# Eight loads of a decode attention kernel whose last bytes go as DMAs of fewer rows

## The chip, the core and the metric

The kernel runs on one core of one Trainium2 chip. The metric is the device time of one execution in microseconds, the median of several runs. Lower is better.

## The reference

Two attention blocks are computed for one decoded token, and their results are mixed by a gate. Block A has 16 heads with a K and a V cache each; block B has 16 query heads that share 8 K and V heads. Each cache is 8192 positions by 256 numbers, all in float32. The query is x (448 numbers) times wq, and the heads' outputs go through wo back to 448 numbers.

```python
def _A_ref(x, k_cache, v_cache, wq, wo):
    q = (x @ wq).reshape(B, Sq, H, Dh).transpose(0, 2, 1, 3)
    scores = jnp.einsum("bhqd,bhkd->bhqk", q, k_cache) * (Dh ** -0.5)
    p = _softmax(scores, axis=-1)
    o = jnp.einsum("bhqk,bhkd->bhqd", p, v_cache)
    return o.transpose(0, 2, 1, 3).reshape(B, Sq, H * Dh) @ wo

# Eight loads of a decode attention kernel whose last bytes go as DMAs of fewer rows
g = _sigmoid((x * gate_w).sum(-1, keepdims=True))
return g * _A_ref(x, ...) + (1 - g) * _B_ref(x, ...)
```

Each byte of the caches and weights is used once, so all 432 MB have to come from HBM into SBUF.

## The kernel before, in words

The host lays all caches and weights into one array, `stream`, in the order in which they are used. There are eight steps s. A step handles two heads of A (r = 0 and 1) and one K and V head of B (r = 2) with its two query heads. `order()` writes the order of the items by hand: wq of a step, four K tiles and four V tiles for each r, and wo. A tile is 128 partitions by 4096 numbers.

The stream is cut without regard to the items into 54 loads (`fills()`): 52 of `FILL` = 15872 numbers (63488 bytes) a partition, and two at the end (`TAIL`) that are cut into four pieces each, of 5632, 4096, 4096 and 1920, and of 1344, 896, 336 and 112 numbers. A `UNIT` is 512 numbers, 2048 bytes. `load(n)` takes a tile from a ring of three slots (`SLOTS`) and issues one DMA for each piece from SyncE (SP). Each piece lies in HBM as one contiguous block, row by row: the block's row p goes to partition p. A new load is issued as soon as the last item that reads the oldest slot has been handled, so SP waits for the last reader of the slot. SP issues nothing else but the output at the end.

The consumers take an item by `pieces()`, which splits it where a load or a piece of a load ends; each split item needs one instruction for each part.

- `scores_a` (K of A): VectorE (DVE) multiplies the tile by the broadcast query in place (L234) and sums over 256 numbers (L235).
- `scores_b` (K of B), `queries` (wq), `attend` (V) and `emit` (wo): TensorE (PE) matmuls, all of them by the helper at L96.
- `softmax`, `take` and `narrow` are short steps on all engines after a head's last tile.

After the last item the kernel adds up the last output row: `emit_last` copies Y, the last blocks of matmuls follow, and the result goes to HBM from four partitions in one DMA of 4 rows (L412).

A DMA has one of eight completion counters, taken in turn. The ninth DMA waits on SP until the first has landed, and so on.

In the profile the load is L112, and its tile is `slot<-in_stream_dram`.

Of the kernel before, what the change touches and what calls it, by code (L numbers as in the profile page):

```python
# [14 lines left out]
P = 128  # L15
# [13 lines left out]
UNIT = 2 * DH  # L29
# [2 lines left out]
WO = 4 * 2 * D  # L32
FILL = 31 * UNIT
SLOTS = 3
TAIL = [[11 * UNIT, 8 * UNIT, 8 * UNIT, 2 * UNIT + 896], [1344, 896, 336, 112]]


def order():

    out = [("wq", 0, 0, 0)]  # L40
    for s in range(NS):
        def k(r, *ts):
            return [("k", s, r, t) for t in ts]

        def v(r, *ts, of=s):
            return [("v", of, r, t) for t in ts]

        if s == 0:
            out += k(0, 0) + k(2, 0, 1) + k(0, 1) + k(2, 2) + k(0, 2) + k(2, 3) + k(0, 3)
            out += v(2, 0, 1) + k(1, 0) + v(2, 2, 3) + k(1, 1) + v(0, 0, 1) + k(1, 2) + v(0, 2)  # L50
            out += k(1, 3) + v(0, 3) + [("wq", 1, 0, 0)]
            continue
        out += k(0, 0) + v(1, 0, 1, of=s - 1) + k(0, 1) + v(1, 2, 3, of=s - 1)
        out += k(0, 2) + k(2, 0, 1) + k(0, 3) + k(2, 2, 3) + [("wo", s - 1, 0, 0)]
        out += k(1, 0) + v(0, 0, 1) + k(1, 1) + v(0, 2, 3)
        if s < NS - 1:
            out += [("wq", s + 1, 0, 0)] + k(1, 2) + v(2, 0, 1) + k(1, 3) + v(2, 2, 3)
        else:
            out += k(1, 2) + v(2, 0) + k(1, 3) + v(2, 1, 2, 3) + v(1, 0, 1, 2, 3) + [("wo", s, 0, 0)]
    return out  # L60
# [5 lines left out]
def fills():  # L66

    total = sum(SIZE[i[0]] for i in order())
    tail = sum(map(sum, TAIL))
    full, rest = divmod(total - tail, FILL)  # L70
    return [[FILL]] * full + ([[rest]] if rest else []) + TAIL


@with_exitstack
def kernel(
# [6 lines left out]
    nc = tc.nc  # L82
    scale = DH ** -0.5

    const = ctx.enter_context(tc.tile_pool(name="const", bufs=1))
    ring = ctx.enter_context(tc.tile_pool(name="ring", bufs=SLOTS))
    small = ctx.enter_context(tc.tile_pool(name="small", bufs=2))
# [9 lines left out]


    FILLS = fills()
    starts, at = [], 0  # L100
    for f in FILLS:
        starts.append(at)
# [4 lines left out]
    def load(n):  # L107
        t = ring.tile([P, FILL], F32, name="slot")
        o = 0
        for size in FILLS[n]:  # L110
            a = (starts[n] + o) * P
            nc.sync.dma_start(t[:, o:o + size], stream[a:a + size * P].rearrange("(p f) -> p f", p=P))  # L112
            o += size
        slots[n] = t

    def pieces(a, n):

        got, end, o = [], a + n, a
        for k, s in enumerate(starts):
            e = s + sum(FILLS[k])  # L120
            if s <= o < e and o < end:
                c = s
                for size in FILLS[k]:
                    if c <= o < c + size and o < end:
# [8 lines left out]
    xs = const.tile([P, 2 * (KF + 1)], F32, name="xs")  # L133
    nc.scalar.dma_start(xs, small_in)
    load(0)
    load(1)
    load(2)

    zero = const.tile([P, UNIT], BF16, name="zero")
# [4 lines left out]
    rows = const.tile([P, 2 * R, NG], F32, name="rows")  # L144
# [24 lines left out]
    for h in range(2):  # L169
        p = slice(h * KR, (h + 1) * KR)  # L170
# [188 lines left out]
    items, a = [], 0  # L359
# [3 lines left out]
    assert a == TOTAL  # L363
    ends = [s + sum(f) for s, f in zip(starts, FILLS)]
    later = {}
# [3 lines left out]

    nxt = SLOTS  # L370
    gone = 0
    last = len(items) - 1
    for i, ((kind, s, r, t), a) in enumerate(items):
# [29 lines left out]
        while gone < len(ends) and a + SIZE[kind] >= ends[gone]:  # L403
            gone += 1
            if nxt < len(FILLS):
                load(nxt)
# [81 lines left out]
```

## Time and profile before

| what | value |
|---|---|
| median of 3 runs | 1013.41 us (1013.23 to 1015.39) |
| the profiled execution | 1013.38 us |
| its span, first to last instruction | 1011.6 us |
| HBM read | 432.02 MB, 427 GB/s over the span |
| busy: PE, DVE, ACT | 535.4, 597.7, 37.6 us |
| DMA packets on SP's queue | 8648, 98.9% of 16 engines' span |
| a full load, from issue to landing, median | 40.4 us |

The profile has a page of sums, the groups of instructions with what ended the idle time before them, the chain of waits that ended last, and, for any stretch of time, the mean busy share of the core's 16 DMA engines and the packets that started in it. A DMA's packets are its rows, and one completion of 4 bytes for each engine that it uses. The packets are not told apart by engine.

### The profile page before, as it was taken

What the parts mean: (1) busy time and instruction counts of PE and PEld (TensorE: products, weight loads), DVE (VectorE), ACT (ScalarE), POOL (GpSimd) and SP (SyncE); (2) the same over time, 40 slices, a digit from 0 to 9 for tenths busy, and PEclk for the clock granted to TensorE, in tenths of its full rate; (3) what the DMA queues carried; (4) which work ended last, traced back from release to release, by engine and by line L of the source; (5) the groups of instructions that cost most, each with busy time, mean ns of one, the idle gap of its engine ahead of it and who ended that gap; (6) DMA issues with size and microseconds to landing.
All of it is one profiled execution on the core that took longest, in us unless ns stands there. A gap on an engine that the chain in (4) does not pass through costs nothing.

```text
span 1011.6 us, 6308 instructions
## 1 busy us (share of the span) xinstructions
PE 535.4 (53%) x2839; PEld 156.0 (15%) x2839; DVE 597.7 (59%) x298; ACT 37.6 (4%) x106; POOL 0.7 (0%) x6
## 2 busy tenths in 40 slices
PE   1715555764628455547325565438554457336647
PEld 0201111120102120112101121102211112102102
DVE  1687775636763488536657635844488447656671
ACT  0000000000000000000000000000000000000000
POOL 0000000000000000000000000000000000000000
PEclk9957776876768676778767877767777778766769
DMA  9999999999999999999999999999999999999996
GB/s 402 440 442 425 422 437 439 437 427 427 434 435 440 429 427 429 437 432 432 432 437 432 428 437 430 435 432 427 437 440 427 425 434 437 437 429 432 427 424 262
DMA packets 8818, 432.42 MB, mean 427 GB/s; under 512 B 1240, under 2 KB 1368, under 8 KB 1752
## 3 DMA queue, kind: packets, MB, share of 16 engines
q1 hardware_dynamic: 8648, 432.02, 98.9%
q8 instruction: 22, 0.36, 0.1%
q10 hardware_dynamic: 144, 0.00, 0.0%
q14 instruction: 4, 0.03, 0.0%
HBM read 432.02 MB, written 0.00 MB: 427 GB/s over the span
## 4 chain that ended last, share of the span: by engine, by line
DMA 62%; DVE 24%; PE 11%; another core or an unknown queue 1%; ACT 1%; issue 0%; SPq 0%
DMA slot<-in_stream_dram 62%; DVE s L235 12%; DVE slot L234 12%; PE sc L96 3%; PE o L96 3%; PE sm L96 2%; PE q L96 2%; PE Y L96 2%; ACT px L277 0%; ACT p L286 0%; SPq L112 0%; DVE least L264 0%; ACT bias L272 0%; DVE low L253 0%
## 5 line engine op out<-in xcount | busy, mean ns | idle before, releaser
L234 DVE TENSOR_TENSOR slot<-slot,q 128x4096 f32<-128x4096 f32 (+5 forms) x80 | 284.7, 3559 | 102.0 <-DMA slot<-in_stream_dram 102.0
L235 DVE TENSOR_REDUCE s<-slot 128x16 f32<-128x4096 f32 (+5 forms) x80 | 285.3, 3567 | 2.8
L96 PE MATMUL o<-slot,p 128*2 128x512 f32 x1024 | 177.3, 797 | 189.8 <-DMA slot<-in_stream_dram 189.8
L96 PE MATMUL sc<-slot,qb 128*32 128x512 f32 x512 | 90.2, 820 | 105.7 <-DMA slot<-in_stream_dram 105.4
L96 PE MATMUL o<-slot,pr 128*4 128x512 f32 x512 | 83.8, 777 | 78.3 <-DMA slot<-in_stream_dram 78.3
L96 PEld LDWEIGHTS o<-slot,p 128*2 128x2 f32 x1024 | 28.8, 99 | 317.9 <-DMA slot<-in_stream_dram 211.2
L264 DVE TENSOR_REDUCE least<-sm 1x1 f32<-1x128 f32 (+1 forms) x24 | 5.8, 243 | 109.2 <-PE sm L96 92.0
L96 PE MATMUL Y<-slot,ocs 128*1 128x448 f32 (+3 forms) x178 | 54.6, 501 | 12.3 <-DMA slot<-in_stream_dram 12.0
L330 DVE TENSOR_TENSOR ocs<-sm,rz 128x2 f32<-128x2 f32 (+1 forms) x24 | 3.7, 154 | 76.8 <-PE sm L96 76.8
L96 PEld LDWEIGHTS sc<-slot,qb 128*32 128x32 f32 x512 | 19.9, 142 | 166.9 <-DMA slot<-in_stream_dram 114.1
L96 PE MATMUL q<-slot,xr 128*128 128x512 f32 (+1 forms) x80 | 35.5, 598 | 0.0
L96 PEld LDWEIGHTS o<-slot,pr 128*4 128x4 f32 x512 | 14.1, 100 | 137.6 <-DMA slot<-in_stream_dram 86.8
L316 ACT ACTIVATE ob<-o 128x512 f32<-128x512 f32 (+1 forms) x24 | 14.1, 588 | 534.7 <-PE o L96 534.7
L96 PE MATMUL sc<-slot,xr 128*1 128x512 f32 (+1 forms) x80 | 28.8, 507 | 0.0
L253 DVE TENSOR_REDUCE low<-sc 128x1 f32<-128x512 f32 x8 | 5.5, 688 | 32.5 <-PE sc L96 32.5
L96 PE MATMUL sm<-pick_a,ob 128*128 128x1 f32 x128 | 19.4, 272 | 5.6 <-ACT ob L316 5.6
L96 PEld LDWEIGHTS sm<-pick_a,ob 128*128 128x128 f32 x128 | 18.0, 217 | 19.2 <-ACT ob L316 16.4
L96 PEld LDWEIGHTS q<-slot,xr 128*128 128x128 f32 x80 | 17.0, 222 | 24.0 <-issue 23.5
L290 DVE RECIPROCAL rz<-sm 128x1 f32<-128x1 f32 (+1 forms) x24 | 4.1, 169 | 27.2 <-PE sm L96 27.2
L96 PE MATMUL sm<-ident,low 128*1 128x128 f32 x48 | 10.8, 312 | 17.6 <-DVE low L238 16.8
L96 PEld LDWEIGHTS Y<-slot,ocs 128*1 128x1 f32 x178 | 11.3, 91 | 49.5 <-issue 36.3
L272 ACT ACTIVATE bias<-sm 128x1 f32<-128x1 f32 x24 | 4.1, 171 | 348.5 <-PE sm L96 348.5
(62 smaller groups left out, 132.8 us busy)
## 6 DMA issues: line engine op xcount, KB each, us to landing
slot<-in_stream_dram SPq DMA_DIRECT2D x52, 7936.0 KB, 40.4
slot<-in_stream_dram SPq DMA_DIRECT2D x2, 2048.0 KB, 32.4
slot<-in_stream_dram SPq DMA_DIRECT2D x1, 2816.0 KB
slot<-in_stream_dram SPq DMA_DIRECT2D x1, 960.0 KB, 36.5
slot<-in_stream_dram SPq DMA_DIRECT2D x1, 672.0 KB, 25.7
slot<-in_stream_dram SPq DMA_DIRECT2D x1, 448.0 KB, 26.5
slot<-in_stream_dram SPq DMA_DIRECT2D x1, 168.0 KB, 26.5
slot<-in_stream_dram SPq DMA_DIRECT2D x1, 56.0 KB, 22.2
```

Of the source, the lines that this page charges most:

```text
L96: nc.tensor.matmul(o, l, r, start=start, stop=stop, skip_group_check=True)
L234: nc.vector.tensor_tensor(v, v, q[:, None, :].to_broadcast([P, n, DH]), op=OP.mult)
L235: nc.vector.tensor_reduce(S[s, r][:, t * ROWS + j:t * ROWS + j + n], v, axis=AX.X, op=OP.add)
L253: nc.vector.tensor_reduce(low, sc, axis=AX.X, op=OP.min)
L264: nc.vector.tensor_reduce(least[:, :m], view, axis=AX.XY if r == 2 else AX.X, op=OP.min)
L272: nc.scalar.activation(bias, all_rows, AF.Copy)
L290: nc.vector.reciprocal(rz[:, :m], z[:, :m])
L316: nc.scalar.activation(ob[:, :n], o[:, :n], AF.Copy)
L330: nc.vector.tensor_tensor(ocs[:, :, :m], oc[:, :, :m], RZ.pop((s, r))[:, None, :m].to_broadcast([P, 2, m]), op=OP.mult)
```

## The change

Eight loads, numbers 30, 32, 34 and so on to 44, are now two pieces. In load 30 the second piece is 10 units (20480 bytes a partition), in the seven others it is one unit (2048 bytes). The first piece is a DMA of 128 rows as before. The second is issued as several DMAs over parts of the partitions (`parts()`): one of 112 rows for partitions 0 to 111, and small ones for the last 16 partitions. In load 30 these are four DMAs of 4 rows. In the seven others they are two, of a and 16 - a rows, with a different pair in each: (12, 4), (10, 6), (9, 7), (13, 3), (14, 2), (15, 1), (11, 5). The same bytes reach the same places of the slots.

```diff
+LOW = 4
+SHARE = 10 * UNIT
+PAIRS = [(12, 4), (10, 6), (9, 7), (13, 3), (14, 2), (15, 1), (11, 5)]
...
-    return [[FILL]] * full + ([[rest]] if rest else []) + TAIL
+    out = [[FILL]] * full + ([[rest]] if rest else []) + TAIL
+    for i in range(len(PAIRS) + 1):
+        m = UNIT if i else SHARE
+        out[len(out) - 24 + 2 * i] = [FILL - m, m]
+    return out
+
+
+def parts():
+
+    whole = [(0, P)]
+    n = len(fills())
+    out = [[whole for _ in f] for f in fills()]
+    few = [(0, P - 16)]
+    out[n - 24][1] = few + [(r, LOW) for r in range(P - 16, P, LOW)]
+    for i, (a, b) in enumerate(PAIRS):
+        out[n - 22 + 2 * i][1] = few + [(P - 16, a), (P - 16 + a, b)]
+    return out
...
-        for size in FILLS[n]:
+        for size, rows in zip(FILLS[n], PARTS[n]):
             a = (starts[n] + o) * P
-            nc.sync.dma_start(t[:, o:o + size], stream[a:a + size * P].rearrange("(p f) -> p f", p=P))
+            block = stream[a:a + size * P].rearrange("(p f) -> p f", p=P)
+            for r, m in rows:
+                nc.sync.dma_start(t[r:r + m, o:o + size], block[r:r + m])
             o += size
```

The order of instructions on SP, before, through all loads up to the first piece of the last (behind a tile stand partitions by float32 numbers; x52 says how many such rows follow each other):

```order
L112 DMA slot<-in_stream_dram 128x15872 x52
L112 DMA slot<-in_stream_dram 128x5632
L112 DMA slot<-in_stream_dram 128x4096 x2
L112 DMA slot<-in_stream_dram 128x1920
L112 DMA slot<-in_stream_dram 128x1344
```

and with the change, from load 30 to load 33, with what SP waits for ahead of each (DMAHW0 to DMAHW7 are the eight completion counters, DVE and PE the last readers of the slot):

```order
L134 DMA slot<-in_stream_dram 128x10752 [waits DMAHW4_49,DVE_49,PE_49]
L134 DMA slot<-in_stream_dram 112x5120
L134 DMA slot<-in_stream_dram 4x5120 x4
L134 DMA slot<-in_stream_dram 128x15872 [waits DMAHW5_49,DVE_49,PE_49]
L134 DMA slot<-in_stream_dram 128x15360 [waits DMAHW6_49,DVE_49,PE_49]
L134 DMA slot<-in_stream_dram 112x512 [waits DMAHW7_49]
L134 DMA slot<-in_stream_dram 12x512 [waits DMAHW0_49]
L134 DMA slot<-in_stream_dram 4x512 [waits DMAHW1_49]
L134 DMA slot<-in_stream_dram 128x15872 [waits DMAHW3_49,DMAHW2_49,DMAHW4_49,DVE_49,PE_49]
```

Load 30 is six DMAs and load 32 four, where each was one. The counters come round after eight DMAs, so the three small ones of load 32 wait for DMAs of load 30.

The consumers' side, on DVE, where a K tile of A lies across the border of the two pieces of load 30, before (L225 is the copy of the queries ahead of it):

```order
L225 COPY qb_110<-sm 128x2x2 [waits PE_49]
L234 TENSOR_TENSOR slot<-slot,q 128x4096 [waits DMAHW7_49]
L235 TENSOR_REDUCE s<-slot 128x16 [waits DVE_49]
L234 TENSOR_TENSOR slot<-slot,q 128x4096 [waits DMAHW0_49]
```

and with the change:

```order
L247 COPY qb_110<-sm 128x2x2 [waits PE_49]
L256 TENSOR_TENSOR slot<-slot,q 128x512 [waits DMAHW7_49]
L257 TENSOR_REDUCE s<-slot 128x2 [waits DVE_49]
L256 TENSOR_TENSOR slot<-slot,q 128x3584 [waits DMAHW3_49,DMAHW2_49,DMAHW4_49,DMAHW1_49,DMAHW0_49]
L257 TENSOR_REDUCE s<-slot 128x14 [waits DVE_49]
L256 TENSOR_TENSOR slot<-slot,q 128x4096 [waits DMAHW5_49]
```

One K tile is now read in two parts, of 512 and 3584 numbers a partition. The second waits for the 112-row DMA and the four small ones. DVE has six instructions more in all, PE has the same matmuls.

More of the change, by code (lines that the diff above doesn't have):

```diff
@@ L99 @@
     FILLS = fills()
+    PARTS = parts()
     starts, at = [], 0
```

## The prediction

> **What bounds the kernel now.** I read the page of the profile first, then the busy time by stretches, the chain of waits in order of time, and last the DMA packets of short stretches. The page:
>
> ```profile
> DMA  9999999999999999999999999999999999999996
> L234 DVE TENSOR_TENSOR slot<-slot,q 128x4096 f32<-128x4096 f32 (+5 forms) x80 | 284.7, 3559 | 102.0 <-DMA slot<-in_stream_dram 102.0
> L96 PE MATMUL o<-slot,p 128*2 128x512 f32 x1024 | 177.3, 797 | 189.8 <-DMA slot<-in_stream_dram 189.8
> DMA slot<-in_stream_dram 62%; DVE s L235 12%; DVE slot L234 12%; PE sc L96 3%; PE o L96 3%; PE sm L96 2%; PE q L96 2%; PE Y L96 2%; ACT px L277 0%; ACT p L286 0%; SPq L112 0%; DVE least L264 0%; ACT bias L272 0%; DVE low L253 0%
> ```
>
> The DMA engines are full in 39 of 40 slices, and PE and DVE stand idle before their work until a slot's data is there. Only the last slice is not full. Busy time in a stretch of the middle, and in short stretches of the end (the last two figures of a row are the mean busy share of the 16 DMA engines and GB/s):
>
> ```profile
> 300.00:500.00 200.00, 110.85 (x566) 32.36 (x566) 111.73 (x52) 7.49 (x22) 0.00 (x0) 0.75 1.00 433
> 1000.00:1000.50 0.50, 0.50 (x8) 0.10 (x4) 0.00 (x0) 0.00 (x0) 0.00 (x0) 1.00 0.82 310
> 1000.50:1001.00 0.50, 0.50 (x8) 0.11 (x4) 0.00 (x0) 0.00 (x0) 0.00 (x0) 1.00 0.68 274
> 1001.00:1002.00 1.00, 0.77 (x8) 0.00 (x0) 0.00 (x0) 0.00 (x0) 0.00 (x0) 1.00 0.53 213
> 1002.00:1003.00 1.00, 0.81 (x4) 0.09 (x4) 0.00 (x0) 0.00 (x0) 0.00 (x0) 1.00 0.52 208
> 1003.00:1004.00 1.00, 0.22 (x2) 0.00 (x0) 0.32 (x1) 0.38 (x1) 0.00 (x0) 1.00 0.43 154
> 1004.00:1005.00 1.00, 0.32 (x12) 0.13 (x16) 0.62 (x2) 0.00 (x0) 0.00 (x0) 1.00 0.27 93
> ```
>
> In the middle the share is 1.00: none of the 16 has a gap, and each moves 433/16 = 27.1 GB/s. At the end they don't stop together. 0.53 of 16 is 8.5 engines at work after 1001 us, 0.27 is 4.3 after 1004: some seven were done by 1001, the last handful runs to about 1005. All had equal bytes, so the late ones lost time on the way. Unused from 1000 to 1005 are (0.18 x 0.5 + 0.32 x 0.5 + 0.47 + 0.48 + 0.57 + 0.73) x 16 = 40 engine-us, or 2.5 us for each of 16: **no sharing out of bytes can gain more than 2.5 us**. What the end hangs on, from the chain in order of time:
>
> ```profile
> 965.65 36.49 DMA slot<-in_stream_dram
> 1002.15 0.04 issue
> 1002.19 1.05 PE o L96 x4
> 1004.68 1.63 PE Y L96 x56
> 1008.66 0.28 DVE ys L411
> ```
>
> The DMA issued at 965.65 is the 1920-element one that holds the last V; PE starts on it 0.04 us after its slowest engine's part has landed, at 1002.15. From there to the span's end, 1011.6, stand 9.4 us of dependent work. So the end follows the slowest DMA engine one to one. Each engine works through its queue in order, so bytes taken from it at any earlier point move its last part by their own time.
>
> One thing that takes time from single engines is in the page and in the packets of a 2 us stretch (934 to 936 us):
>
> ```profile
> q8 instruction: 22, 0.36, 0.1%
> q8 instruction: 1, 0.02, 3.5%
> ```
>
> 22 instruction fetches of 16 KB share these engines, and one holds an engine for 3.5% of 16 x 2 us = 1.1 us. Three on one engine and none on another would make 3.4 us of the spread of about 5. Which engines are late no row names.
>
> **The change, part by part.** How many engines a DMA uses can be counted:
>
> ```profile
> q1 hardware_dynamic: 8648, 432.02, 98.9%
> q10 hardware_dynamic: 144, 0.00, 0.0%
> ```
>
> 144 for the one ACT load is 128 rows and 16 completions. SP's 60 loads make 60 x 144 = 8640; the 8 left over are the output DMA, 4 rows and 4 completions. So a DMA of 4 rows went to 4 engines, and I take it that 1 to 15 rows go to as many engines, always the same first ones, while 112 rows give each of 16 seven. In blocks of 2048 bytes, against the eight equal rows of before, the long edit (20480 bytes, ten blocks) gives the first four engines 7 + 4 rows, +30 blocks, and the other twelve 7, -10. A pair (a, 16-a) gives +1 to the engines that are in both small DMAs and -1 to those in neither. Summed over the seven pairs: +37, +36, +35, +34 for the first four, -7, -8, -9 and then -10, -10 and -11 down to -17 for the others; the sum is 0.
>
> *Bytes.* A block costs 2048 / 27.06 = 0.0757 us. An engine among the twelve is relieved of 7 to 17 blocks, 0.53 to 1.29 us, with a mean of 142/12 = 11.8 blocks, 0.90 us. One of the four takes up 34 to 37, 2.6 to 2.8 us. The early engines have the room: at least the three that stopped before 1000.5 and about four more before 1001 lead the last by 4 us and more.
>
> *More packets.* Each edited load gives each engine 7 more row packets and 1 more completion, so 8 x 8 = 64 on an engine of the twelve, and about 36 more for one of the four (4 rows and 4 completions, 14 and 14). The shortest packets are those of the last DMA, in the stretch from 1004.7 to 1005.0 us:
>
> ```profile
> DMA packets 32, 0.02 MB, mean 55 GB/s; under 512 B 27, under 2 KB 32, under 8 KB 32
> q1 hardware_dynamic: 32, 0.02, 18.6%
> ```
>
> 0.186 x 16 x 0.3 / 32 = 28 ns each, for 55 GB/s x 0.3 us / 32 = 516 bytes, 19 ns at full rate: up to 9 ns of overhead. From below it is 0, if a packet's start overlaps the last one's end. 64 packets cost 0 to 0.57 us; I take 0.4. One of the four pays 0 to 0.9, I take 0.6.
>
> *SP.* 26 more DMAs are issued, 18 of them small, and the waits on their numbered completion counters come with them:
>
> ```profile
> slot<-in_stream_dram SPq DMA_DIRECT2D x52, 7936.0 KB, 40.4
> slot<-in_stream_dram SPq DMA_DIRECT2D x2, 7936.0 KB, 35.5
> L112 SPq DMA_DIRECT2D slot<-in_stream_dram x60: 327/328/433, 0.7 to 983.3; - x60
> ```
>
> An issue is 0.33 to 0.43 us; four more are 1.7 us. From issue to landing pass 40.4 us in the median (35.5 in the stretch from 900 to 990 us), of which 7936 x 1024 bytes / 433 GB/s = 18.8 us are its own transfer: 16 to 22 us of cover. The new waits (load 32's small DMAs on those of load 30) end when load 30 has landed; load 31's 18.8 us still lie ahead of them. Behind them on SP stands only load 33, which waits for the slot of load 30 in any case. Price 0; without the cover, the issue time of 1.7 us a load.
>
> *Consumers.* DVE's half tiles are cut further at the new borders: three more pairs of instructions. Cost by form:
>
> ```profile
> L234 DVE TENSOR_TENSOR slot<-slot,q 128x4096 f32<-128x4096 f32 x48 | 211.8, 4412 | 67.5 <-DMA slot<-in_stream_dram 67.5
> L234 DVE TENSOR_TENSOR slot<-slot,q 128x512 f32<-128x512 f32 x2 | 1.4, 684 | 2.2 <-DMA slot<-in_stream_dram 2.2
> ```
>
> Per 512 elements the slope is (4412 - 684)/7 = 533 ns, so a cut adds 151 ns an instruction, 0.9 us for six, hidden in DVE's waits for data; if DVE bounded, it would be +0.9. In return the first part of a cut load is free to be read before the rest is there. Nothing of this reaches the end: the last load that is cut is the tenth from the last, and the final 9.4 us of work are as before.
>
> **Sum**: slowest engine -0.9 + 0.4 = -0.5 us, from 1.3 faster (17 blocks, free packets) to 0.04 slower (7 blocks, dear packets). The profiled execution took 1013.38 us (span 1011.6), the median is 1013.41, so the same base: **1012.9 us**, its own range 1012.0 to 1013.6.
>
> [...]
>
> **The rivals.**
>
> *The receivers are late ones.* If one of the first four is among the handful at work after 1004, it ends 34 to 37 blocks, 2.7 us, and 0.6 of packets later: +3.3, **1016.7 us**. For it: nothing here says who is late, and 0.52 of 16, about eight, still work 2 us after the first seven are done. Against it: if late engines are neighbours, as a set of eight that the fetches visit in turn might be, either half is as good. It decides from a receiver that is less than 2.8 us ahead of the last.
>
> *Rows that enter SBUF by one door.* In every DMA of before an engine writes rows that no other engine writes at that time, and the steady 1.00 at 433 GB/s tells nothing of two that meet. The four rows of a small DMA are neighbours, written by four engines at once. If such a group of four partitions takes in no more than one engine delivers, 27 GB/s, a DMA of 4 x 20480 bytes lasts 4 x 0.757 = 3.0 us, not 0.76, and four of them 12.1, not 3.0: +9.1 us on the four engines; the 14 small ones up to 14 x 3 x 0.0757 = +3.2. The four would end 2.7 + 0.6 + 12.3 = 15.6 us later than their 1000.5, at 1016, 11 after today's last: **1024 us**, more if the 112-row DMAs meet too (their split no longer fits that of 128 rows): up to twice the loss, 1034. It decides from 1.2 us of collisions, which is the lead of 4.5 (1000.5 to 1005) less the 3.3 they already take. Against it stands only that queues of engines that are out of step collide less.
>
> [...]
>
> *Nothing is moved.* Small DMAs that take another set of engines each time spread their rows, and only packets remain: +0.4, **1013.8 us**. For it: the one DMA of 4 rows in the trace shows four engines, not which.
>
> **How the numbers follow.** Forecast 0.55, receivers late 0.13, one door 0.19, nothing moved 0.10, and 0.03 that engines even out far better than the blocks say. What a measurement here can tell from no change is 0.2%, 2.0 us. Faster by that needs 2.0 of the 2.5 us bound: 0.03. Within it fall the forecast and "nothing moved": 0.65. Slower: 0.32. The range 1012.0 to 1018.0 holds the forecast, the late receivers, the unmoved case and the mild end of the one door, together about 0.8.
>
> **What would show it.** Right: the share in 1-us stretches before the end falls later and more steeply (0.53 becomes about 0.75, since four engines now end near 1003.5), and the last V's landing comes some 0.5 us before 1002.15. Late receivers: a share of at most 0.25 over the last 3 us. One door: GB/s under 430 from load 30 on (about 580 us), and 4-row DMAs that land long after the 112-row one. Wrong altogether, if PE or DVE idle grows by more than the end moves, or SP waits on landings for longer than 16 us.

## The result: 2.6% slower

The changed kernel takes 1040.16 us (median; 1037.54 to 1040.87) against 1013.32 us of the kernel before beside it: a ratio of 1.0256, 95% interval 1.0243 to 1.0268, or 26.8 us. The profiled execution took 1039.82 us with a span of 1038.0, 26.4 us more than before. The forecast of 1012.9 and its range up to 1018.0 were wrong.

### The profile page after: what moved, and what is told of

Its sections match the earlier page's. It is cut to its first block, busy times and chain, and to the rows that moved or that the text cites. A ratio compares the mean times of both kernels' runs of the same rounds, so it can differ in the third digit from the quotient of the medians.

```text
span 1038.0 us, 6365 instructions
## 1 busy us (share of the span) xinstructions
PE 531.4 (51%) x2839; PEld 157.3 (15%) x2839; DVE 598.5 (58%) x304; ACT 37.6 (4%) x106; POOL 0.7 (0%) x6
## 3 DMA queue, kind: packets, MB, share of 16 engines
q1 hardware_dynamic: 9928, 432.02, 98.9%
## 4 chain that ended last, share of the span: by engine, by line
DMA 59%; DVE 21%; PE 15%; ACT 2%; another core or an unknown queue 1%; issue 1%; SPq 0%; DVEq 0%
DMA slot<-in_stream_dram 57%; DVE slot L256 10%; DVE s L257 10%; PE Y L115 5%; PE o L115 4%; PE sc L115 3%; PE sm L115 2%; DMA xs<-in_small_dram 2%; PE q L115 1%; ACT px L299 1%; DVE pr L301 0%; ACT p L308 0%; DVE least L286 0%; DVE low L275 0%
## 5 line engine op out<-in xcount | busy, mean ns | idle before, releaser
L256 DVE TENSOR_TENSOR slot<-slot,q 128x4096 f32<-128x4096 f32 (+6 forms) x83 | 285.1, 3435 | 124.3 <-DMA slot<-in_stream_dram 124.3
L257 DVE TENSOR_REDUCE s<-slot 128x16 f32<-128x4096 f32 (+6 forms) x83 | 285.8, 3443 | 2.9
L115 PE MATMUL sc<-slot,qb 128*32 128x512 f32 x512 | 86.7, 791 | 108.6 <-DMA slot<-in_stream_dram 108.3
L115 PE MATMUL q<-slot,xr 128*128 128x512 f32 (+1 forms) x80 | 32.7, 559 | 0.0
```

The lines of the kernel that those rows point to most:

```text
L115: nc.tensor.matmul(o, l, r, start=start, stop=stop, skip_group_check=True)
L256: nc.vector.tensor_tensor(v, v, q[:, None, :].to_broadcast([P, n, DH]), op=OP.mult)
L257: nc.vector.tensor_reduce(S[s, r][:, t * ROWS + j:t * ROWS + j + n], v, axis=AX.X, op=OP.add)
```

## The profile after

The page of the changed kernel, the same lines as were read of before (DMA share and GB/s in 40 slices of 26 us, the queue of the loads, the two largest groups of consumers):

```profile
DMA  9999999999999999999999999999999999999996
GB/s 399 445 439 432 431 431 431 431 431 431 438 431 431 431 434 438 431 432 433 436 433 420 264 394 404 422 405 405 430 409 399 431 412 407 431 431 433 431 417 252
q1 hardware_dynamic: 9928, 432.02, 98.9%
L256 DVE TENSOR_TENSOR slot<-slot,q 128x4096 f32<-128x4096 f32 (+6 forms) x83 | 285.1, 3435 | 124.3 <-DMA slot<-in_stream_dram 124.3
L115 PE MATMUL o<-slot,p 128*2 128x512 f32 x1024 | 176.3, 792 | 195.2 <-DMA slot<-in_stream_dram 195.2
```

The bytes are the same, and the DMA engines are as "full" as before. What differs is the second line: 431 GB/s and more from slice 2 to slice 21, then 264 in slice 23 (571 to 597 us) and 394 to 431 in the eleven after it. DVE and PE are no busier; they wait longer for the slots. That hole and one later stretch, in stretches of time (PE, PEld, DVE, ACT, POOL busy, then granted clock, share of the 16 DMA engines, GB/s):

```profile
300.00:500.00 200.00, 109.08 (x564) 33.01 (x565) 111.80 (x51) 7.29 (x21) 0.00 (x0) 0.75 1.00 434
570.00:575.00 5.00, 5.00 (x28) 0.88 (x24) 4.96 (x3) 0.00 (x0) 0.00 (x0) 0.53 1.04 447
575.00:580.00 5.00, 1.56 (x14) 0.18 (x6) 5.00 (x2) 0.00 (x0) 0.00 (x0) 1.00 0.97 328
580.00:585.00 5.00, 0.00 (x0) 0.00 (x0) 4.96 (x2) 0.00 (x0) 0.00 (x0) 0.65 1.00 222
585.00:590.00 5.00, 4.48 (x26) 0.81 (x26) 0.13 (x1) 0.00 (x0) 0.00 (x0) 0.66 1.36 235
590.00:595.00 5.00, 5.00 (x15) 2.05 (x14) 0.00 (x0) 0.60 (x1) 0.00 (x0) 1.00 0.99 129
595.00:600.00 5.00, 4.63 (x25) 2.45 (x23) 0.49 (x3) 0.59 (x1) 0.00 (x0) 1.00 0.87 207
600.00:605.00 5.00, 1.06 (x6) 0.13 (x6) 4.96 (x3) 0.00 (x0) 0.00 (x0) 0.70 0.91 395
630.00:640.00 10.00, 0.00 (x0) 0.00 (x0) 0.00 (x0) 0.00 (x0) 0.00 (x0) 0.64 0.99 350
```

The kernel before, in the middle of that time:

```profile
585.00:590.00 5.00, 2.13 (x12) 0.40 (x16) 0.00 (x0) 0.00 (x0) 0.00 (x0) 0.50 0.97 419
```

From 575 to 600 us, while load 30's second piece passes, the engines carry 129 to 328 GB/s with a share of 0.87 to 1.36. A share of 1 with half the bytes is no empty queue: packets are under way and take twice as long. (A packet's whole time counts in the stretch in which it starts; so the share can pass 1.) At 630 to 640, around load 32's 2048-byte piece, it is 350.

Two readings were worked out from the packet records, and they come back below. The **lag** is the time at which a kernel has moved a number of bytes, less the time at which the kernel before had moved as many. In the changed kernel it is 0.1 us up to 557 us, 12.9 after load 30, then grows by 1.4 to 1.9 with each of the seven other loads, to 25.4 us. The **packet times**: a row of 20480 bytes takes 0.765 us in a DMA of 128 rows (in the last load of the kernels with extra bytes, below), but 1.5 us (median) in load 30's second piece, 2.2 to 3.1 us in the 4-row DMAs, and whole rows of 43008 to 63488 bytes that are under way at the same time take up to 7.8 us, where 2.35 is normal.

The end, in order of time, of the chain of waits (start, length, what):

```profile
989.11 38.46 DMA slot<-in_stream_dram
1027.62 1.05 PE o L115 x4
1030.10 1.63 PE Y L115 x56
1034.43 0.27 DVE ys L433
```

It is the same chain, 25.4 us later: V has landed at 1027.6 in place of 1002.2. From there to the end of the span it is 10.4 us in place of 9.4. The last microseconds of the transfers:

```profile
1026.00:1027.00 1.00, 1.00 (x12) 0.10 (x4) 0.00 (x0) 0.00 (x0) 0.00 (x0) 1.00 0.72 292
1027.00:1028.00 1.00, 0.59 (x6) 0.10 (x4) 0.00 (x0) 0.00 (x0) 0.00 (x0) 1.00 0.72 282
1028.00:1029.00 1.00, 0.64 (x4) 0.00 (x0) 0.00 (x0) 0.31 (x1) 0.00 (x0) 1.00 0.55 185
1029.00:1030.00 1.00, 0.00 (x0) 0.00 (x0) 0.90 (x2) 0.07 (x1) 0.00 (x0) 1.00 0.09 33
```

The share falls later and more steeply than before: 0.72, 0.72, 0.55, 0.09 against 0.53, 0.52, 0.43, 0.27. By the last eight rows of each engine, eleven of the 16 end within 2 us (1027.4 to 1029.4), where before all 16 were spread over 5 (999.9 to 1005.1). Four end earlier, at 1024.6 to 1025.8, and one at 1030.5, as an instruction fetch fell on it at 1029.0. So most engines came closer together, but the last V lands 25.4 us later, just as far as the stream had fallen behind: nothing was gained at the end.

## The experiments

The theory after the result: rows that neighbouring engines write into the same few partitions enter SBUF by a shared entrance ("door"), so that any split of a DMA by rows that makes engines meet there costs time. Its rivals: the change made the engines uneven (the receivers became the late ones); more DMAs cost, through SP's issues, completion counters and packets; the HBM side reads worse; or any DMA of other than 128 rows is slow, whatever its partitions. Each time below has the kernel before beside it; that took 1013.1 to 1013.8 us. A split is written as (first row, rows), later as (first row, rows, step), in the run cut along the columns as (first column, columns). Only the lines of an edit that matter are shown; `load()` and the layout on the host follow them. "..." stands for lines left out.

**The two parts apart.** Load 30 alone:

```diff
-PAIRS = [(12, 4), (10, 6), (9, 7), (13, 3), (14, 2), (15, 1), (11, 5)]
+PAIRS = []
```

> The change's cut of load 30 alone (112 rows and four DMAs of 4 rows, 20480 bytes each row); the seven pairs are left out. All theories: the trace of the change lags that of before by 14.7 us when the first 280 MB are through, before the second pair has come, and some 1 to 2 us of that belong to the first pair, so this kernel should be 13 to 15 us slower than before, some 1027. If the loss of the change were one thing that needs all eight cut loads together (the rings of completion counters, for example), it would be under 5 us.

Measured: 1024.07 us, ratio 1.0100 [1.0079, 1.0121], +11.0 us, where 13 to 15 had been expected; lag 11.8. The seven other loads alone:

```diff
-        m = UNIT if i else SHARE
-        out[len(out) - 24 + 2 * i] = [FILL - m, m]
+        if i:
+            out[len(out) - 24 + 2 * i] = [FILL - UNIT, UNIT]
...
-    out[n - 24][1] = few + [(r, LOW) for r in range(P - 16, P, LOW)]
```

> The seven pairs alone (112 rows and two small DMAs of 2048 bytes a row); load 30 is whole. The lag of the change grows by 1.4 to 1.9 us at each pair, so 7 x 1.6 = about 11 us slower than before, 1024, on the theory of doors (engines that write rows of one group of partitions share its way in). On the theory that the loss comes from four engines that carry too much, nothing is lost here, since a pair moves 2048 bytes at most: within 1 us of before.

Measured: 1023.70 us, 1.0096 [1.0076, 1.0116], +10.6 us; lag 10.95, 1.56 for each of the seven. Both parts lose. The pairs move no more than 2048 bytes to or from an engine each, so bytes in the wrong place can't make 1.56 us a load, whose block is 0.076 us. The two sums give 21.5 of 26.8 us. Of the other 5, the trace shows 1.1 us more lag at load 30 and 1.5 more at the pairs when both are there, and 1 us more after V's landing, and what V gained on the stream in each part alone (0.2 and 0.4 us) is gone; why the parts cost more together was not tried.

**As many DMAs, without a split by rows.** The same pieces, the same number of DMAs in each load, but all of 128 rows and cut along the columns (5 x 1024 numbers; 256, 128 and 128):

```diff
-    few = [(0, P - 16)]
-    out[n - 24][1] = few + [(r, LOW) for r in range(P - 16, P, LOW)]
-    for i, (a, b) in enumerate(PAIRS):
-        out[n - 22 + 2 * i][1] = few + [(P - 16, a), (P - 16 + a, b)]
+    out = [[[(0, s)] for s in f] for f in fills()]
+    out[n - 24][1] = [(c * 2 * UNIT, 2 * UNIT) for c in range(5)]
+    for i in range(len(PAIRS)):
+        out[n - 22 + 2 * i][1] = [(0, UNIT // 2), (UNIT // 2, UNIT // 4), (3 * UNIT // 4, UNIT // 4)]
```

> The same eight loads are cut at the same places and into as many DMAs as in the change (six for load 30, four for each of the seven others), but every DMA has all 128 rows and a part of the columns. So SP issues and waits as often, there are more and shorter packets, and each engine carries equal bytes to its usual rows. Doors: no loss beyond the packets, 0 to 1 us. Waits and counters of SP, or the cut itself and its packets: the loss of the change, some 26 us, would stay.

Measured: 1014.80 us, 1.0017 [1.0007, 1.0026], +1.7 us, at this number of packets:

```profile
q1 hardware_dynamic: 12392, 432.02, 99.1%
```

That is 12392 - 8648 = 3744 packets more than before, 234 for an engine, and the lag is 1.94 us: 8.3 ns a packet, if all of it is put down to them. SP's issues and waits, the counters and the consumers' cuts are all in this kernel, so together they cost no more than this. The change has 64 to 100 more packets an engine, so 0.5 to 0.8 of its 26.8 us.

**The same bytes for every engine.** From here to the extra bytes, load 30 alone is cut (`PAIRS = []`). Its last 16 rows as one DMA:

```diff
-    out[n - 24][1] = few + [(r, LOW) for r in range(P - 16, P, LOW)]
+    out[n - 24][1] = [(0, P - 16, 1), (P - 16, 16, 1)]
```

> Load 30 alone is cut, as 112 rows and one DMA of 16 rows of 20480 bytes: 7 + 1 rows for each of 16 engines, so all engines carry equal bytes again. Uneven engines: no loss, within 1 us of before. Doors: the 112 rows collide as in the change (their packets took about 1.5 us there against 0.76 at full rate, 5 us over 7 rows), and 16 neighbouring rows on four groups make 4 engines share one, 2.3 us more: 6 to 9 us slower than before.

Measured: 1023.33 us, 1.0092 [1.0072, 1.0113], +10.2 us, where 6 to 9 had been expected; lag 10.7. In the hole:

```profile
580.00:585.00 5.00, 0.42 (x4) 0.11 (x8) 4.97 (x2) 0.00 (x0) 0.00 (x0) 0.50 1.01 226
585.00:590.00 5.00, 5.00 (x25) 0.85 (x18) 2.83 (x1) 0.00 (x0) 0.00 (x0) 0.50 1.18 222
590.00:595.00 5.00, 5.00 (x14) 1.94 (x13) 0.00 (x0) 0.60 (x1) 0.00 (x0) 0.98 1.25 243
```

Nothing is moved from one engine to another (7 + 1 rows each), and the hole is there. With that the late receivers fall as its cause.

**Which partitions meet.** Now load 30's 20480 bytes are eight DMAs of 16 rows, one row for each engine in each; only the choice of rows differs. Neighbours:

```diff
-    out[n - 24][1] = few + [(r, LOW) for r in range(P - 16, P, LOW)]
+    out[n - 24][1] = [(r, 16, 1) for r in range(0, P, 16)]
```

> Load 30 alone: its last 20480 bytes a row go as eight DMAs of 16 neighbouring rows. Every engine carries eight rows, as before, and there are no more packets than with one DMA of 128 rows but for seven completions. Doors (groups of four neighbouring partitions, 16 of them in all): 16 neighbouring rows reach four doors, four engines to each, so a row takes 4 x 0.757 us and eight rows 24 us instead of 6: up to 18 us slower, 14 if engines out of step use other doors meanwhile. Uneven engines: no loss. Cost of small DMAs: under 1 us, and the same as in the next run.

Every eighth row:

```diff
+    out[n - 24][1] = [(r, 16, 8) for r in range(8)]
```

> As the run with eight DMAs of 16 neighbouring rows, but each DMA takes every eighth row (partitions i, i+8, ... i+120), in HBM as in SBUF. Same engines, bytes, packets and DMAs. Doors: 16 such rows reach eight doors, two engines to each: about 6 us slower than before, a third of the run with neighbouring rows. If the number of DMAs or packets or their size counts, it is as slow as that run.

Measured: 1028.32 us, 1.0142 [1.0121, 1.0162] with neighbours, 1023.65 us, 1.0096 [1.0075, 1.0116] with every eighth row, where 14 to 18 and about 6 us more than before had been expected; lags 13.9 and 9.7. The packets take 1.89 and 1.51 us (median). The hole with neighbours, and then with every eighth row:

```profile
580.00:585.00 5.00, 0.00 (x0) 0.00 (x0) 4.96 (x2) 0.00 (x0) 0.00 (x0) 0.67 1.01 174
585.00:590.00 5.00, 3.07 (x16) 0.55 (x20) 0.24 (x1) 0.00 (x0) 0.00 (x0) 0.50 1.04 184
```

```profile
580.00:585.00 5.00, 0.00 (x0) 0.00 (x0) 4.96 (x2) 0.00 (x0) 0.00 (x0) 0.50 0.96 198
585.00:590.00 5.00, 3.89 (x20) 0.69 (x24) 2.74 (x1) 0.00 (x0) 0.00 (x0) 0.50 1.09 234
```

Same bytes, engines and packets, and 4.7 us between them: the partitions matter. But neighbours cost 1.4 times as much, not the three times that engines in lockstep would make: engines that have fallen out of step would write rows of different DMAs, and so use other doors. That reason is argued, not shown.

An estimate from the rate of one engine here, 27.06 GB/s: if two engines share one entrance, 16 engines write through eight, at 8 x 27.06 = 216 GB/s, and the rows show 198 to 234 for every eighth row, with packets of 1.51 us, twice the 0.765 of a DMA of 128 rows. If four share one, 16 neighbours write through four, at 108, and the rows show 174 to 184; there the measurement differs, and engines out of step would explain it.

**Every second row of 32**, so that the 16 rows lie within 32 neighbouring partitions:

```diff
+    out[n - 24][1] = [(h + i, 16, 2) for h in range(0, P, 32) for i in range(2)]
```

> As the run with eight DMAs of 16 rows, but each takes every second partition of a group of 32. It tells which partitions share a door. [...] If a door were simply eight neighbouring partitions, 32 of them would reach four, four engines to each: as 16 neighbouring rows or slower, 14 us.

Measured: 1023.62 us, 1.0100 [1.0081, 1.0118], lag 9.6, packets 1.52 us: the same as every eighth row. Groups of eight neighbours would have made this one as dear as 16 neighbours. Groups of four neighbours alone would have made every eighth row free, since its 16 rows lie in 16 of them. Both runs fit groups of four neighbouring partitions of which two, in different blocks of 32, share an entrance. Within partitions 0 to 31 no two seem to: eight groups there were written at once in packets of 0.765 us (own groups, below). By this estimate the 32 groups of 128 partitions have 16 entrances, and every eighth row reaches eight, the 216 GB/s of above; which groups belong together no run shows. "Group" means four neighbouring partitions from here on.

**The HBM side.** As every eighth row, but laid out in HBM in the order in which the DMAs read:

```diff
-                nc.sync.dma_start(t[r:e:k, o:o + size], block[r:e:k])
+                nc.sync.dma_start(t[r:e:k, o:o + size], block[i * m:(i + 1) * m])
```

> As the run with every eighth partition, but the block lies in HBM in the order in which the DMAs read it, so each reads 16 neighbouring rows from HBM and writes every eighth partition. If the loss is made where SBUF is written (doors): as the run with every eighth row, some 6 us. If it is made by neighbouring rows read from HBM: as the run with 16 neighbouring rows, 14 to 18 us.

Measured: 1023.44 us, 1.0094 [1.0073, 1.0114], against 1023.65. Whether the rows of a DMA lie together in HBM or not makes no difference.

**Small DMAs spread.** The 112 rows of the change, and four DMAs of every fourth of the last 16 rows:

```diff
+    out[n - 24][1] = [(0, P - 16, 1)] + [(P - 16 + i, 4, 4) for i in range(4)]
```

> The cut of load 30 alone, as in the run with the share alone (112 rows and four DMAs of 4 rows; that was 11 us slower than before), but each small DMA takes every fourth of the last 16 partitions, so its four rows reach four doors instead of one. Same engines, bytes and DMAs. If neighbouring rows in the small DMAs make a large part of the loss: 3 to 5 us slower than before instead of 11. If nearly all of it is made by the 112 rows: 9 to 11 us.

Measured: 1022.44 us, 1.0088 [1.0070, 1.0107], lag 9.3 against 11.8 with neighbours. Neighbouring rows in the small DMAs make 2.5 us; the larger part of load 30's loss is elsewhere.

**Two that settled little.** The last 6144 bytes as 16 DMAs of 8 rows, each row in a group of its own:

```diff
-SHARE = 10 * UNIT
+SHARE = 3 * UNIT
...
+    out[n - 24][1] = [(h + i, 8, 4) for h in (0, 32, 64, 96) for i in range(4)]
```

> Load 30 alone: its last 6144 bytes a row go as sixteen DMAs of 8 rows, every fourth partition from h + i on (h = 0, 32, 64, 96; i = 0 to 3). Eight engines carry 16 rows of it and the other eight none, 8 x 6144 bytes = 49 KB or 1.8 us moved from eight engines to the other eight, without any DMA of 112 rows, and in each small DMA every engine has a door of its own. If a door takes no more than one engine delivers, the engines relieved lose at their doors what they are spared: the end stays within 0.5 us where they are the late ones, and comes up to 3.8 us later where the receivers are. If a door takes more than that and the relieved ones are late: up to 1.8 us faster. Uneven engines alone: 1.8 us faster or 2.0 slower, and which tells on which half the late engines are.

Measured: 1023.46 us, 1.0095 [1.0078, 1.0112]. It is late for another reason:

```profile
580.00:585.00 5.00, 0.00 (x0) 0.00 (x0) 4.51 (x2) 0.00 (x0) 0.00 (x0) 0.54 0.64 269
585.00:590.00 5.00, 3.88 (x20) 0.69 (x24) 0.00 (x0) 0.00 (x0) 0.00 (x0) 0.50 0.15 46
590.00:595.00 5.00, 5.00 (x19) 1.84 (x11) 0.00 (x0) 0.60 (x1) 0.00 (x0) 0.93 0.75 254
```

Here the share falls to 0.15: the queue is empty. Seventeen DMAs on eight counters make SP wait until the load's first DMAs have landed, and no cover is left. The gaps are (0.36 + 0.85 + 0.25) x 5 = 7.3 us of its 9.7. Its packets took 241 ns in the median, 6144 bytes at full rate being 227, but they are of two kinds: the 64 to partitions 0 to 63 took 232 to 288 ns, the 64 to partitions 64 to 127 took 232 to 459, with a median of 336, though each was alone in its group and the queue was all but empty. No run here shows why. And every eighth row at half the size:

```diff
-SHARE = 10 * UNIT
+SHARE = 5 * UNIT
```

> As the run with every eighth row (9.7 us slower than before), with 10240 bytes a row instead of 20480. Two engines to a door double the time of the piece: 6.1 us more for 20480 bytes, 3.0 for 10240. If the loss is all proportional to the bytes that collide: 4.9 us slower. If some 3.6 us of it are a fixed price for each disturbed load (engines that come out of step): 6.6 us.

Measured: 1020.92 us, 1.0073 [1.0055, 1.0092], lag 6.1 against 9.7. Nine DMAs in the load let the queue run short here too (a share of 0.43 for 5 us, 2.9 us), so what remains, about 3, can't be told from half of 9.7 with some error.

**Extra bytes, to price a DMA by itself.** The next four kernels start from the kernel before and cut no load by rows. Load 30 takes 10752 numbers a partition, the 5120 columns that are free in its slot take extra bytes that nothing reads, and the last load carries what was put off:

```diff
-    return [[FILL]] * full + ([[rest]] if rest else []) + TAIL
+MORE = 10 * UNIT
...
+    out = [[FILL]] * full + ([[rest]] if rest else []) + TAIL
+    out[len(out) - 24] = [FILL - MORE]
+    out[-2] = [11 * UNIT, 8 * UNIT, 8 * UNIT, 2 * UNIT]
+    out[-1] = [MORE, 896] + out[-1]
+    return out
```

The yardstick, four DMAs of all rows (c = MORE // 16):

```diff
+            nc.sync.dma_start(t[:, i * c:i * c + c], stream[:P * c].rearrange("(p f) -> p f", p=P))
```

> A yardstick. Load 30 of the kernel before takes 10752 numbers a partition, and the 5120 columns of the slot that this leaves free take extra bytes, which nothing reads: four DMAs of 128 rows by 320 numbers (1280 bytes), 0.655 MB. The 5120 numbers of the stream that are put off go to the last load, which so is 8704 numbers in six pieces. Each theory: 0.655 MB / 433 GB/s = 1.5 us later from load 30 on, 32 row packets of about 8.3 ns more on each engine (0.3 us), so +1.8 us at equal bytes; the end may shift by a few us in either direction because the last loads are cut otherwise, alike in the next kernels.

Four of 8 rows, each row in a group of its own:

```diff
+            nc.sync.dma_start(t[i:32:4], stream[:8 * MORE].rearrange("(p f) -> p f", p=8))
```

> The same, but the extra bytes are four DMAs of 8 rows by 5120 numbers, DMA i on partitions i, i + 4, ... i + 28: again 0.655 MB, on eight engines, each of them in a group of four neighbouring partitions of its own. Doors: no two engines of a DMA share a group, so these packets take 0.76 us each; eight engines are 4 x 0.757 = 3.0 us later than the others, and the mean over all is 1.5 us, as with all rows: within 2 us of the yardstick. That anything but 128 rows costs, whatever the partitions: as with neighbouring rows in the next kernel, packets of 1.5 us and longer, and whole-row packets of the neighbours held up.

Four of 8 neighbouring rows:

```diff
+            nc.sync.dma_start(t[8 * i:8 * i + 8], stream[:8 * MORE].rearrange("(p f) -> p f", p=8))
```

> The same four DMAs of 8 rows by 5120 numbers, on partitions 0 to 7, 8 to 15, 16 to 23 and 24 to 31: same bytes, same engines, same number of packets as the one before. Doors: four engines in each group of four at once, packets of about 3 us, 4 x 3.0 = 12.1 us on the eight engines in place of 3.0, a mean of 6 us over all 16 engines, and whole-row packets of the same groups held up beside: 6 to 12 us over the kernel before it. That only the number of rows matters: the same time as the kernel before it, within 1 us.

One of 112 rows:

```diff
+        nc.sync.dma_start(t[:112], stream[:112 * MORE].rearrange("(p f) -> p f", p=112))
```

> The same place, one DMA of 112 rows by 5120 numbers (2.29 MB): the first DMA of the changed load 30, alone and beside the whole stream. Its bytes are 7 x 0.757 = 5.3 us on each engine, 3.8 more than the yardstick's. Doors: seven rows an engine cross the groups of eight, so two engines meet in most groups, and the whole-row packets behind them are held up: some 9 us more than its bytes, as the run with 112 rows and spread small DMAs had over the kernel before, so about 12.5 to 13 us over the yardstick. That the loss of load 30 comes from its small DMAs: 3.8 us over the yardstick.

Measured (the lag is at equal bytes, so the extra bytes are out of it; packets of 20480 bytes and the longest whole-row packet from 560 to 640 us, from the records):

```
                    time us   ratio to before            lag us   20480 B: median (range) us    longest whole row us
all rows            1016.01   1.0035 [1.0022, 1.0047]     0.3      -                             3.0
own groups          1016.92   1.0043 [1.0028, 1.0058]     0.1      0.765 (0.761 to 0.769)        3.0
neighbours          1021.80   1.0086 [1.0069, 1.0102]     3.4      1.38  (0.81 to 2.05)          4.8
112 rows            1027.86   1.0147 [1.0132, 1.0162]     8.1      1.49  (0.81 to 2.05)          4.5
```

The stretch from 580 to 585 us, for own groups:

```profile
580.00:585.00 5.00, 3.15 (x16) 0.55 (x20) 4.96 (x2) 0.00 (x0) 0.00 (x0) 0.50 1.05 451
```

for neighbours:

```profile
580.00:585.00 5.00, 1.12 (x8) 0.26 (x12) 4.89 (x2) 0.00 (x0) 0.00 (x0) 0.60 1.10 298
```

and for 112 rows:

```profile
580.00:585.00 5.00, 0.00 (x0) 0.00 (x0) 4.96 (x2) 0.00 (x0) 0.00 (x0) 0.50 1.03 211
```

This pair decides. Four DMAs of 8 rows, equal in bytes, number of engines, packets and counters, go at full rate with each row in a group of its own, not one of 32 packets longer than 0.769 us, and fall to 298 GB/s when the eight rows are neighbours. So it isn't the number of rows that costs but the partitions that the engines write at once, and the runs of 16 rows say which: those of one group, and of groups in different blocks of 32 that share an entrance. The size was overrated: 4.9 us between the two, where 6 to 12 were expected, since the packets took 1.4 us and not 3. And one 112-row DMA alone costs 8.1 us beyond its bytes (11.85 over the yardstick, where 3.8 are bytes and 12.5 to 13 were expected): it is the larger part of load 30's 11.8.

**A version that beats both.** The dependent work behind the last V, 9.4 us, has steps that don't need the last bytes. Y's copy is taken one step earlier, and the last `narrow` comes one block earlier, after five of the last eight:

```diff
         elif s < NS - 1:
             emit(s, a)
+            if s == NS - 2:
+                emit_last(s, a)
...
-            emit_last(s, a)
             todo = list(blocks(s, a))
-            for b, l in todo[:6]:
+            for b, l in todo[:5]:
                 emit_block(b, l)
             narrow(s, 1)
-            for b, l in todo[6:]:
+            for b, l in todo[5:]:
                 emit_block(b, l)
```

> The kernel before, with its loads as they were; only the end of the work is put in another order. The copy of Y and its four matmuls go ahead, to the last output block of the step before, and the narrow step of the last head stands after five of the eight last blocks instead of six. From the chain at the end: the copy and its matmuls (0.61 + 0.3 us and 0.3 of issue) no longer stand between the last V and the output, and the blocks run while ACT copies: 1.0 to 1.6 us faster than before, 0.1 to 0.16%, if the data of the last load are there in time (1004.96 and 1005.38 us in the profile); if they are what is waited for, 0.5 us or less.

Measured: 1011.19 us (1011.06 to 1011.39), 0.9977 [0.9968, 0.9986]: 2.2 us faster than the kernel before, with its loads unchanged; 1.0 to 1.6 had been expected. The end of its chain of waits:

```profile
978.96 24.85 DMA slot<-in_stream_dram
1003.85 0.76 PE Y L96 x24
1004.61 0.98 PE sm L96 x8
1005.59 0.89 PE Y L96 x24
1006.50 0.28 DVE ys L412
```

V no longer ends the chain. It now runs through the last pieces of wo, which land 1.7 us later, and behind them stand 5.6 us of work in place of 9.4.

## Why the prediction was wrong, step by step

- **What bounds the kernel**: right. DVE and PE do the same work as before and wait longer for the slots, and the end follows the transfers: V lands 25.4 us later, and the span ends 26.4 later.
- **Bytes**: this is the step that failed. It priced every row at its bytes over 27.06 GB/s, wherever it goes: 0.757 us for 20480 bytes, 0.0757 for 2048. That rate was read from the kernel before, whose loads are all DMAs of 128 rows, and the step took it over to 112 rows and to small DMAs of neighbours. A row of load 30's second piece took 1.5 us, and in the 4-row DMAs 2.2 to 3.1. The lag of the whole stream from these splits is 25.4 us, in place of 0.
- **The relief itself**: also wrong. 0.9 us had been put down. Against the stream, the last V gained 0.2 us with load 30 alone (it lands 11.55 us later at a lag of 11.8), 0.4 with the pairs alone, and nothing in the change (25.4 us later at a lag of 25.4). The share at the end is as forecast (0.72 for "about 0.75"), so most engines did come closer together, but the slowest one's part did not land earlier for it.
- **The engines of a DMA**: their number was right. SP's 9928 packets are 60 x 144 + 8 + 8 x 128 + 4 x 8 + 7 x 32: a completion for each of 16 engines with 112 rows, and for as many engines as rows with 1 to 15. That these are always the same first ones was an assumption; no record names an engine.
- **More packets**: right. At most 8.3 ns each by the kernel cut along columns, between the bounds of 0 and 9; the 0.4 us taken could have been 0.53.
- **SP at price 0**: right for this change: the same number of DMAs in 128-row form costs 1.7 us with all its packets. Its cover is not endless: with nine or 17 DMAs in a load the queue ran short (a share of 0.43 and of 0.15 over 5 us).
- **Consumers**: right. DVE has 598.5 us of work against 597.7 and waits 124.3 us for data against 102.0.
- **The rival "one door"** is what happened, by its first sign: under 430 GB/s in the stretches from load 30 on that hold a cut load (350 from 630 to 640 us). Its chance of 0.19 was too low for a case against which only the queues' being out of step was brought. Its condition, that four neighbouring partitions take in no more than one engine delivers, was shown by no row of before; by it four engines that meet would need 3.0 us a row, and the rows of the 4-row DMAs took 2.2 to 3.1, those of four DMAs of 8 neighbours 1.38. Its price was too low as well, 1024 and at most 1034. It charged the small DMAs' four engines alone (9.1 + 3.2 us) and doubled that loss for the 112-row DMAs. The runs put it the other way round: the 112-row DMA makes 8.1 us of load 30's 11.8 by itself, the neighbouring rows of the small ones 2.5. It also left out the whole rows that the engines beside carry: the records of the changed kernel hold 7.8 us an engine of excess in the 20480-byte packets, 1.7 in the 2048-byte ones and 16.6 in the whole rows of the same and the next load. And the rival counted on the four engines' lead of 4.5 us to swallow part, while the loss fell on all 16.
- **Late receivers, nothing moved**: neither makes the loss. Load 30 with equal bytes for all engines still loses 10.2 us.

Still open is which engine takes which of the 112 rows, since no record names the engine; that the 112-row DMA loses by the same meeting of engines is inferred from its packet times and its 211 GB/s, not shown by a 112-row DMA that avoids it. Open too is why the loss is larger than two engines' sharing of one entrance would make it, and whether the engines of one DMA meet each other or the whole rows of other loads that are under way, which no run tells apart. The one split that moved bytes between engines and kept each in a group of its own (6144 bytes in 16 DMAs) let the queue run empty, so what such a relief is worth is not shown.

## What to carry to other kernels

A full DMA rate is the rate of one pattern, here of DMAs of 128 rows (27.06 GB/s an engine, 0.765 us for 20480 bytes, against 1.49 us in a DMA of 112 rows); before a load is split by rows, price the split by a run with that DMA as extra bytes. If a piece must be smaller, cut it along the columns, at 8 ns a packet and 1.7 us for eight loads here, and keep all 128 rows. Few rows went at full rate here only where each of a DMA's eight rows was in a group of its own within one block of 32, and all of them only in partitions 0 to 63. And look at GB/s beside the busy share: here full engines with half the bytes (a share of 1.01 at 174 GB/s) were held up, and a low share (0.15 at 46 GB/s) was an empty queue, and the two have different cures.

## What had not been expected of the hardware

- The whole stream pays for a meeting of few engines. In the changed kernel, packets of 63488 bytes that had nothing to do with the cut took up to 7.8 us in place of 2.35. Whether they stood behind the cut rows or only shared a way in with them, no run shows.
- A 2048-byte piece split by rows costs 1.56 us a load (10.95 over seven), twenty times what one row of it takes.
- An instruction fetch (16 KB on q8, 22 of them in all) delays its engine by 1.07 us in the median, and in the kernel before the next whole row took 0.46 to 0.55 us longer than its 2.35. Each engine's packets follow each other without a gap (in the median a packet starts 4 ns before the one ahead ends), and followed so, the fetches visit eight engines in turn. By 1003 us there had been 21 in the kernel before, three on each of five engines and two on each of three, and the ends fit: five at 1004.6 to 1005.1 us, three at 1003.0 to 1003.5, the other eight at 999.9 to 1002.0. So the late engines were those with fetches, which the prediction could not name. One such fetch in the last 2 us gave the changed kernel its last engine.
